# Block-diagonal attention keys: two masked copies in place of one broadcast product

## The chip, the cores and the metric

The kernel runs on one core of a Trainium2 chip. The metric is device time in microseconds (us), the median of three runs. A profiled execution gives the span of the program and, for each engine, what it did and waited for. TensorE does matmuls, VectorE and ScalarE work on what the matmuls leave in PSUM, GpSimd works on SBUF, and SyncE issues transfers. In the profile they are called PE (PEld for its weight loads), DVE, ACT, POOL and SP.

## The reference

The program normalises 2048 rows of 512 numbers and adds three things: the rows themselves, a sliding-window attention with 32 heads of only 16 numbers each, and a gated layer whose two hidden products of 1792 are multiplied with each other.

```python
def _A_ref(x, wqkv, wo):
    B, S, D = x.shape
    H = 32; Dh = D // H; W = 256
    # q, k, v: [B, H, S, Dh] from x @ wqkv
    scores = jnp.einsum("bhqd,bhkd->bhqk", q, k) * (Dh ** -0.5)
    mask = (idx[:, None] - idx[None, :] >= 0) & (idx[:, None] - idx[None, :] < W)
    scores = jnp.where(mask[None, None], scores, -1e9)
    p = _softmax(scores, axis=-1)
    o = jnp.einsum("bhqk,bhkd->bhqd", p, v)
    return (o back to [B, S, D]) @ wo

def _B_ref(x, w_gate, w_up, w_down):
    return ((x @ w_gate) * (x @ w_up)) @ w_down

xn = _layernorm(x)
return x + _A_ref(xn, A_wqkv, A_wo) + _B_ref(xn, B_w_gate, B_w_up, B_w_down)
```

(Shortened: the two returns and the comment put in words or in one line what the reference spells out with einsum and reshape.)

## The kernel before

The rows are worked on in four chunks T of 512. Within a chunk, the 32 heads are in four groups c of eight, so that one projection of 128 output partitions holds eight heads of 16. Partitions 0 to 15 belong to the first head of a pair, 16 to 31 to the second, and so on.

The score matmuls work on 32 partitions, that is, on a pair of heads, and must not mix the two. For this the keys are laid out block-diagonally: for each block of 64 key positions the tile K has 128 columns, 64 for the first head of the pair and 64 for the second. Where the column belongs to one head, the partitions of the other head are zero. The mask is made once, at the start:

```python
podd = const.tile([128, 1], I32, name="podd")          # L104: (partition >> 4) & 1
nc.vector.tensor_scalar(out=podd[:], in0=pi[:], scalar1=4, scalar2=1,
                        op0=ALU.arith_shift_right, op1=ALU.bitwise_and)
self.pair = const.tile([128, 2], BF16, name="pair")     # column 0: even, column 1: odd
nc.vector.tensor_copy(out=self.pair[:, 1:2], in_=podd[:])
nc.vector.tensor_scalar(out=self.pair[:, 0:1], in0=self.pair[:, 1:2], scalar1=-1.0, scalar2=1.0,
                        op0=ALU.mult, op1=ALU.add)
```

The projection of queries and keys, sixteen times of each kind (four chunks, four groups):

```python
def proj_qk(self, T, c, is_k, ks=range(4), engine=None):
    ps = self.bank(ks, "qkp")                            # one PSUM bank, 128 x 512 f32
    for k in ks:
        nc.tensor.matmul(ps[:], ...)                     # L254
    if 3 not in ks:
        return
    if is_k:
        self.K[T, c] = self.kpool.tile([128, 1024], BF16, tag="K", name="K")
        k = self.work.tile([128, 512], BF16, tag="k", name="k")
        self.copy(k[:], ps[:], engine)                   # PSUM to SBUF; frees the bank
        nc.vector.tensor_tensor(                         # L262
            out=self.K[T, c].rearrange("p (j r n) -> p j r n", r=2, n=64), op=ALU.mult,
            in0=k.rearrange("p (j n) -> p j n", n=64).unsqueeze(2).to_broadcast([128, 8, 2, 64]),
            in1=self.pair.unsqueeze(1).unsqueeze(3).to_broadcast([128, 8, 2, 64]))
        self.book("dve", BOTH)
    else:
        self.Q[T, c] = self.qpool.tile([128, 512], BF16, tag="Q", name="Q")
        self.copy(self.Q[T, c][:], ps[:], engine)
```

Where the engine is not given, `copy` decides between ScalarE (L233) and VectorE (L235) from a book of costs that the program keeps while it is being built. `BOTH` is an entry of that book. It changes nothing on the chip directly, but it can change which engine a later copy is given to:

```python
EXP, MASK, BOTH, SUMS, DIVIDE, TURN, STATS = 8.7, 1.9, 2.9, 4.2, 8.2, 6.1, 4.2
COPY = dict(act=2.8, dve=3.2)

def copy(self, out, in_, engine=None):
    if engine is None:
        engine = min(COPY, key=lambda e: max(self.free[e], self.now) + COPY[e])
    self.book(engine, COPY[engine])
    if engine == "act":
        nc.scalar.activation(out=out, in_=in_, func=ACT.Copy)    # L233
    else:
        nc.vector.tensor_copy(out=out, in_=in_)                  # L235
```

Those who use the keys, and the others that matter here:

```python
# scores: 75 steps; K is the stationary operand, four pairs of heads at once
nc.tensor.matmul(S[:, e, col:col + n], lhsT=self.K[U, c][rows, keys], rhs=self.Q[T, c][rows, q:q + n], ...)   # L315
nc.scalar.activation(out=P[:, :, 0:col], in_=S[:, :, 0:col], func=ACT.Exp, scale=0.25)                        # L321
# the window's edge is cut on GpSimd (L161), the diagonal on VectorE:
self.nc.vector.tensor_tensor(out=v, in0=v, op=ALU.min, in1=self.diag...)                                      # L345
# values: two accumulators, each one PSUM bank
accs = [self.ps_m.tile([128, 512], F32, tag="M", name="acc") for _ in range(2)]
nc.tensor.matmul(accs[par][...], lhsT=v, rhs=P[rows, e, col:col + n], ...)                                    # L368
```

The pool `ps_m` has four PSUM banks, which projections, gate and up products (L397, L408), down products (L430, L436) and accumulators take in turn. S has the other four, as a single buffer. The order in which TensorE works is laid down by hand: score steps are spread evenly among the projections and the gated layer.

Of the kernel before, what the change touches and what calls it, by code (L numbers as in the profile page):

```python
# [7 lines left out]
BF16 = mybir.dt.bfloat16  # L8
F32 = mybir.dt.float32
I32 = mybir.dt.int32  # L10
ACT = mybir.ActivationFunctionType
ALU = mybir.AluOpType
# [16 lines left out]
PADS = {27: 110, 57: 150}  # L29
MASKED, FIRST_DIVIDE, SECOND_DIVIDE = 8, 8, 24  # L30
COPY = dict(act=2.8, dve=3.2)
EXP, MASK, BOTH, SUMS, DIVIDE, TURN, STATS = 8.7, 1.9, 2.9, 4.2, 8.2, 6.1, 4.2


class Kernel:
# [26 lines left out]
    def setup(self):  # L62
        nc, const, NT, NF = self.nc, self.const, self.NT, self.NF
        self.x = const.tile([128, NT, 512], BF16, name="x")
        self.Wqkv = const.tile([128, 4, 1536], BF16, name="Wqkv")
        self.Wo = const.tile([128, 4, 512], BF16, name="Wo")
        self.Wg = const.tile([128, 4, self.F], BF16, name="Wg")
        self.Wu = const.tile([128, 4, self.F], BF16, name="Wu")
        self.Wd = const.tile([128, NF, 512], BF16, name="Wd")
        xv = self.x_d.rearrange("(t p) d -> p t d", p=128)  # L70
        wq = self.w_d["qkv"].rearrange("(k p) n -> p k n", p=128)
        wg = self.w_d["g"].rearrange("(k p) n -> p k n", p=128)
        wu = self.w_d["u"].rearrange("(k p) n -> p k n", p=128)
        for lo, hi in ((0, 1), (1, 2), (2, 4)):
            nc.sync.dma_start(out=self.x[:, lo:hi, :], in_=xv[:, lo:hi, :])
        for lo in (1024, 512, 0):
            nc.sync.dma_start(out=self.Wqkv[:, :, lo:lo + 512], in_=wq[:, :, lo:lo + 512])
        h = self.F // 2
        for lo in (0, h):
            nc.sync.dma_start(out=self.Wg[:, :, lo:lo + h], in_=wg[:, :, lo:lo + h])  # L80
            nc.sync.dma_start(out=self.Wu[:, :, lo:lo + h], in_=wu[:, :, lo:lo + h])
            if lo == 0:
                nc.sync.dma_start(out=self.x[:, 4:8, :], in_=xv[:, 4:8, :])
        nc.sync.dma_start(out=self.Wd[:], in_=self.w_d["d"].rearrange("(f p) n -> p f n", p=128))
        wo = self.w_d["o"].rearrange("(c p) n -> p c n", p=128)
        for c in range(4):
            nc.sync.dma_start(out=self.Wo[:, c, :], in_=wo[:, c, :])
        for lo, hi in ((8, 10), (10, 12), (12, NT)):
            nc.sync.dma_start(out=self.x[:, lo:hi, :], in_=xv[:, lo:hi, :])

        warm = const.tile([128, 1], F32, name="warm")
        nc.vector.memset(warm[:], 0.0)
        nc.scalar.activation(out=warm[:], in_=warm[:], func=ACT.Exp)
        self.idle = const.tile([128, 128], BF16, name="idle")
        nc.vector.memset(self.idle[:], 0.0)
        self.keep_busy(40)
        ident = const.tile([128, 128], BF16, name="ident")
        nc.gpsimd.memset(ident[:], 0.0)
        nc.gpsimd.affine_select(out=ident[:], in_=ident[:], compare_op=ALU.not_equal, fill=1.0,
                                base=0, pattern=[[-1, 128]], channel_multiplier=1)  # L100
        self.ident = ident
        pi = const.tile([128, 1], I32, name="pi")
        nc.gpsimd.iota(pi[:], pattern=[[0, 1]], base=0, channel_multiplier=1)
        podd = const.tile([128, 1], I32, name="podd")  # L104
        nc.vector.tensor_scalar(out=podd[:], in0=pi[:], scalar1=4, scalar2=1,
                                op0=ALU.arith_shift_right, op1=ALU.bitwise_and)
        self.pair = const.tile([128, 2], BF16, name="pair")
        nc.vector.tensor_copy(out=self.pair[:, 1:2], in_=podd[:])
        nc.vector.tensor_scalar(out=self.pair[:, 0:1], in0=self.pair[:, 1:2], scalar1=-1.0, scalar2=1.0,
                                op0=ALU.mult, op1=ALU.add)  # L110
        self.mhalf = const.tile([128, 4], F32, name="mhalf")
        nc.gpsimd.memset(self.mhalf[:], -0.5)
        self.diag = const.tile([128, 64], BF16, name="diag")
        self.far = const.tile([128, 64], BF16, name="far")
        nc.gpsimd.memset(self.diag[:], BIG)
        nc.gpsimd.memset(self.far[:], BIG)
        for half in (slice(0, 64), slice(64, 128)):
            self.triangle(self.diag[half], True)
            self.triangle(self.far[half], False)
        self.xnT, self.Q, self.hT, self.OT = {}, {}, {}, {}  # L120
        self.K, self.V, self.VS = {}, {}, {}
        self.strips, self.parts, self.at = {}, {}, {}
        self.stock = []
        self.new_values()
# [124 lines left out]
    def proj_qk(self, T, c, is_k, ks=range(4), engine=None):  # L249
        nc = self.nc  # L250
        lo = 512 * is_k + 128 * c
        ps = self.bank(ks, "qkp")
        for k in ks:
            nc.tensor.matmul(ps[:], lhsT=self.Wqkv[:, k, lo:lo + 128], rhs=self.xnT[T][:, :, k, :],  # L254
                             start=(k == 0), stop=(k == 3))
# [3 lines that stand above are left out]
            self.K[T, c] = self.kpool.tile([128, 1024], BF16, tag="K", name="K")  # L259
            k = self.work.tile([128, 512], BF16, tag="k", name="k")  # L260
            self.copy(k[:], ps[:], engine)
            nc.vector.tensor_tensor(out=self.K[T, c].rearrange("p (j r n) -> p j r n", r=2, n=64), op=ALU.mult,  # L262
                                    in0=k.rearrange("p (j n) -> p j n", n=64).unsqueeze(2).to_broadcast([128, 8, 2, 64]),
                                    in1=self.pair.unsqueeze(1).unsqueeze(3).to_broadcast([128, 8, 2, 64]))
            self.book("dve", BOTH)
        else:
            self.Q[T, c] = self.qpool.tile([128, 512], BF16, tag="Q", name="Q")
            self.copy(self.Q[T, c][:], ps[:], engine)
# [404 lines left out]
```

## Time and profile before

| | before |
|---|---|
| median of three runs | 264.81 us (264.8 to 265.33) |
| span of the profiled execution | 263.1 us |
| mean granted TensorE clock | 0.999 |
| the key product (L262) | 16 times, 20.1 us of VectorE, 1262 ns mean |
| the matmul of 128x512 (L397) | 224 times, 380 ns mean in the record, one every 0.216 us (0.86 us for four) |
| PSUM copies on VectorE (L235, 128x512) | about 0.68 us each |
| PSUM copies on ScalarE (L233, 128x512) | about 0.60 us each |
| the exponential (L321) | 75 times, 1877 ns mean |

How to read it: the busy time of an engine is the time in which at least one of its instructions ran. Matmuls overlap in the records, which is why a single one lasts longer than the distance between two. A line such as `PE acc L368 <- DVE Q L235: 0.6, 1, 0.6` tells that the matmuls of line 368 waited for the VectorE instruction of line 235 that writes Q: 0.6 us in total, once, 0.6 us at the longest. In a timeline a line begins with the start and the length in us, and ends, in brackets, with the idle time of the engine before it and what ended it.

### The profile page before, as it was taken

Reading aid. Unit: us, or ns where it says so; the run is one execution under the profiler, and the core shown is the slowest. Engines: PE = TensorE matmul, PEld = TensorE weight load, DVE = VectorE, ACT = ScalarE, POOL = GpSimd, SP = SyncE. Lnnn points to the kernel's source line nnn. Section 1 sums busy time; section 2 is a strip of 40 time slices with the busy share of each in tenths; the row PEclk is TensorE's granted clock in tenths of the full one; section 3 lists DMA queues with packets and bytes.
Section 4 is the critical chain, followed back from the end, with each engine's and each line's share of the span. In section 5 each row is a group of like instructions: output and inputs, shape, how many; then the busy total and the mean of one; then the engine's idle time right before and its main releaser. Section 6 shows DMA issues by size and latency. Waiting matters only on the chain.

```text
span 263.1 us, 7719 instructions
## 1 busy us (share of the span) xinstructions
PE 257.9 (98%) x3170; PEld 118.5 (45%) x3170; DVE 187.9 (71%) x341; ACT 176.7 (67%) x143; POOL 123.8 (47%) x278
## 2 busy tenths in 40 slices
PE   8999999998999999999999999999999999999995
PEld 8434444443443544344544454434543445444453
DVE  6698888879945597568983759767995235977344
ACT  3477788888656876778776566867787546787500
POOL 6217342427456745237556644544664451464600
PEclk9999999999999999999999999999999999999999
DMA  6999921120002300002001310000100100000002
GB/s 204 376 354 340 265 29 20 24 47 1 2 20 42 100 5 0 4 0 47 2 2 40 82 41 5 0 0 16 36 2 0 42 21 22 5 0 2 1 2 82
DMA packets 19427, 15.05 MB, mean 57 GB/s; under 512 B 7360, under 2 KB 19392, under 8 KB 19392
## 3 DMA queue, kind: packets, MB, share of 16 engines
q1 hardware_dynamic: 18848, 14.26, 18.9%
q8 instruction: 26, 0.43, 0.7%
q10 hardware_dynamic: 544, 0.30, 0.4%
q14 instruction: 9, 0.07, 0.1%
HBM read 9.70 MB, written 2.10 MB: 45 GB/s over the span
## 4 chain that ended last, share of the span: by engine, by line
PE 94%; DVE 4%; issue 1%; ACT 0%
PE up L408 19%; PE gp L397 19%; PE psd L430 17%; PE S L315 9%; PE qkp L254 8%; PE acc L368 6%; PE vp L242 5%; PE psd L436 5%; PE L L430 2%; PE wps L130 2%; DVE K L262 1%; DVE k L235 1%; PE L L436 1%; DVE P L345 1%; PE L L368 0%
## 5 line engine op out<-in xcount | busy, mean ns | idle before, releaser
L321 ACT ACTIVATE P<-S 128x2048 bf16<-128x2048 f32 x75 | 140.8, 1877 | 50.2 <-PE S L315 43.2
L161 POOL TENSOR_SCALAR_AFFINE_SELECT P<-P 64x256 bf16<-64x256 bf16 x224 | 107.2, 479 | 117.7 <-ACT P L321 99.1
L397 PE MATMUL gp<-xnT,Wg 128*128 128x512 bf16 x224 | 60.1, 380 | 0.0
L408 PE MATMUL up<-xnT,Wu 128*128 128x512 bf16 x224 | 59.1, 380 | 0.0
L413 DVE TENSOR_TENSOR hT<-up,gsb 128x512 bf16<-128x512 f32 x56 | 38.2, 684 | 16.4 <-PE up L408 11.9
L430 PE MATMUL psd<-Wd,hT 128*128 128x512 bf16 (+1 forms) x210 | 48.0, 369 | 0.0
L345 DVE TENSOR_TENSOR P<-P,diag 128x512 bf16<-128x512 bf16 (+1 forms) x75 | 30.9, 412 | 5.9 <-ACT P L321 5.9
L430 PEld LDWEIGHTS <-hT 128*128 128x128 bf16 x238 | 21.3, 98 | 25.3 <-issue 3.5
L408 PEld LDWEIGHTS <-Wu 128*128 128x128 bf16 x224 | 20.4, 98 | 25.6 <-issue 3.4
L397 PEld LDWEIGHTS <-Wg 128*128 128x128 bf16 x224 | 20.3, 98 | 25.3 <-issue 3.3
L315 PE MATMUL S<-Q,K 32*128 32x320 bf16 (+4 forms) x720 | 29.9, 254 | 0.3 <-DVE K L262 0.3
L254 PE MATMUL qkp<-xnT,Wqkv 128*128 128x512 bf16 x128 | 29.9, 380 | 0.0
L233 ACT ACTIVATE gsb<-gp 128x512 bf16<-128x512 f32 x39 | 22.9, 597 | 8.1 <-PE gp L397 7.2
L315 PEld LDWEIGHTS <-K 32*128 32x128 bf16 x720 | 10.3, 92 | 31.1 <-issue 30.3
L374 DVE STREAM_TRANSPOSE at<-acc 128x512 f32<-128x512 f32 x30 | 19.1, 686 | 5.2 <-PE acc L368 5.2
L262 DVE TENSOR_TENSOR K<-k,pair 128x1024 bf16<-128x1024 bf16 x16 | 20.1, 1262 | 2.0 <-ACT k L233 1.7
L446 DVE TENSOR_TENSOR x<-psd,x 128x512 bf16<-128x512 f32 (+1 forms) x15 | 9.7, 655 | 15.6 <-PE psd L436 15.6
L254 PEld LDWEIGHTS <-Wqkv 128*128 128x128 bf16 x128 | 11.7, 98 | 14.6 <-issue 1.8
L368 PE MATMUL acc<-P,V 64*32 64x320 bf16 (+4 forms) x672 | 17.7, 253 | 0.6 <-DVE Q L235 0.6
L368 PE MATMUL acc<-P,VS 64*32 64x320 bf16 (+4 forms) x672 | 17.7, 253 | 0.4 <-DVE k L235 0.4
L368 PEld LDWEIGHTS <-V 64*32 64x32 bf16 x720 | 15.2, 91 | 2.9 <-issue 2.5
L242 PE MATMUL vp<-Wqkv,xnT 128*128 128x512 bf16 x64 | 15.3, 380 | 0.0
(53 smaller groups left out, 183.1 us busy)
## 6 DMA issues: line engine op xcount, KB each, us to landing
out_dram<-x SPq DMA_DIRECT2D x15, 128.0 KB, 1.9
Wg<-in_B_w_gate_dram SPq DMA_DIRECT2D x2, 896.0 KB, 11.4
Wu<-in_B_w_up_dram SPq DMA_DIRECT2D x2, 896.0 KB, 12.7
Wd<-in_B_w_down_dram SPq DMA_DIRECT2D x1, 1792.0 KB, 17.3
Wqkv<-in_A_wqkv_dram SPq DMA_DIRECT2D x3, 512.0 KB, 6.2
x<-in_A_x_dram SPq DMA_DIRECT2D x2, 512.0 KB, 9.2
VS<-V SPq DMA_DIRECT2D x6, 144.0 KB, 2.6
x<-in_A_x_dram SPq DMA_DIRECT2D x3, 256.0 KB, 6.6
```

The lines of the kernel that those rows point to most:

```text
L161: nc.gpsimd.affine_select(out=v, in_=v, pattern=pattern + [[1 if diag else -1, 64]], compare_op=ALU.is_ge if diag else ALU.is_gt, fill=0.0 ...
L233: nc.scalar.activation(out=out, in_=in_, func=ACT.Copy)
L242: nc.tensor.matmul(ps[:], lhsT=self.xnT[T][:, b, k, :], rhs=self.Wqkv[:, k, 1024:1536], start=(k == 0), stop=(k == 3))
L254: nc.tensor.matmul(ps[:], lhsT=self.Wqkv[:, k, lo:lo + 128], rhs=self.xnT[T][:, :, k, :], start=(k == 0), stop=(k == 3))
L315: nc.tensor.matmul(S[:, e, col:col + n], lhsT=self.K[U, c][rows, keys], rhs=self.Q[T, c][rows, q:q + n], start=True, stop=True, tile_posit ...
L321: nc.scalar.activation(out=P[:, :, 0:col], in_=S[:, :, 0:col], func=ACT.Exp, scale=0.25)
L345: self.nc.vector.tensor_tensor(out=v, in0=v, op=ALU.min, in1=self.diag.unsqueeze(1).unsqueeze(1).to_broadcast([128, 4, n, 64]))
L368: nc.tensor.matmul(accs[par][32 * e:32 * e + 32, q:q + n], lhsT=v, rhs=P[rows, e, col:col + n], start=(i == 0), stop=(i == len(todo) - 1), ...
L397: nc.tensor.matmul(ps[:], lhsT=self.Wg[:, k, 128 * f:128 * f + 128], rhs=self.xnT[T][:, :, k, :], start=(k == 0), stop=(k == 3))
L408: nc.tensor.matmul(ps[:], lhsT=self.Wu[:, k, 128 * f:128 * f + 128], rhs=self.xnT[T][:, :, k, :], start=(k == 0), stop=(k == 3))
L413: nc.vector.tensor_tensor(out=self.hT[T, f][:], in0=ps[:], in1=self.gsb[:], op=ALU.mult)
L430: nc.tensor.matmul(ps, lhsT=self.hT[T, f][:, 128 * b:128 * b + 128], rhs=self.Wd[:, f, c0:c1], start=(f == 0), stop=False)
```

## The change

The product of the keys with a broadcast mask is replaced by two operations with one tensor input each. One multiplies the 512 columns by a per-partition scalar that is 1 for the partitions of even heads and 0 for the others, and writes the first 64 of every 128 columns of K. The other does so with the opposite scalar, for the other 64. What K holds is the same. It is meant to let VectorE do the step with operations that have a single tensor input and no broadcast operand. The two masks are kept as separate float columns, and the entry in the book of costs goes from 2.9 to 3.4.

```diff
-EXP, MASK, BOTH, SUMS, DIVIDE, TURN, STATS = 8.7, 1.9, 2.9, 4.2, 8.2, 6.1, 4.2
+EXP, MASK, BOTH, SUMS, DIVIDE, TURN, STATS = 8.7, 1.9, 3.4, 4.2, 8.2, 6.1, 4.2
@@ setup
-        self.pair = const.tile([128, 2], BF16, name="pair")
-        nc.vector.tensor_copy(out=self.pair[:, 1:2], in_=podd[:])
-        nc.vector.tensor_scalar(out=self.pair[:, 0:1], in0=self.pair[:, 1:2], scalar1=-1.0, scalar2=1.0,
+        self.odd = const.tile([128, 1], F32, name="odd")
+        nc.vector.tensor_copy(out=self.odd[:], in_=podd[:])
+        self.even = const.tile([128, 1], F32, name="even")
+        nc.vector.tensor_scalar(out=self.even[:], in0=self.odd[:], scalar1=-1.0, scalar2=1.0,
                                 op0=ALU.mult, op1=ALU.add)
@@ proj_qk
-            nc.vector.tensor_tensor(out=self.K[T, c].rearrange("p (j r n) -> p j r n", r=2, n=64), op=ALU.mult,
-                                    in0=k.rearrange("p (j n) -> p j n", n=64).unsqueeze(2).to_broadcast([128, 8, 2, 64]),
-                                    in1=self.pair.unsqueeze(1).unsqueeze(3).to_broadcast([128, 8, 2, 64]))
+            pair = self.K[T, c].rearrange("p (j r n) -> p j r n", r=2, n=64)
+            for par, mask in enumerate((self.even, self.odd)):
+                nc.vector.tensor_scalar(out=pair[:, :, par, :], in0=k.rearrange("p (j n) -> p j n", n=64),
+                                        scalar1=mask[:, 0:1], scalar2=None, op0=ALU.mult)
             self.book("dve", BOTH)
```

Built with the new number in the book, four PSUM copies change engines. In the second chunk's projection, a copy of k goes from VectorE to ScalarE and a gate copy from ScalarE to VectorE. In the last chunk's projection, a copy of Q goes from VectorE to ScalarE and a copy of k the other way. The orders of instructions of TensorE and of GpSimd are the same in both kernels.

## The prediction

> **What bounds the kernel now.** I read the shares of busy time first, then the chain, then the waits of TensorE, then the two stretches of the timeline in which such a wait stands.
>
> ```profile
> PE 257.9 (98%) x3170; PEld 118.5 (45%) x3170; DVE 187.9 (71%) x341; ACT 176.7 (67%) x143; POOL 123.8 (47%) x278
> ...
> PE 94%; DVE 4%; issue 1%; ACT 0%
> ```
>
> TensorE is busy for 257.9 of 263.1 us, and 94% of the chain that ended last is matmuls. VectorE, which the change works on, is at 71% and holds 4% of the chain. So the first limit on any gain is the 5.2 us in which TensorE has nothing to do. The waits of TensorE, with columns total us, times, longest us, account for 2.4 of them:
>
> ```profile
> PE wps L130 <- DVE idle L95: 1.1, 1, 1.1
> PE acc L368 <- DVE Q L235: 0.6, 1, 0.6
> PE acc L368 <- DVE k L235: 0.4, 1, 0.4
> PE S L315 <- DVE K L262: 0.3, 1, 0.3
> ```
>
> The first is the start of the program, before any key exists. The rest of the 5.2, about 2.8 us, is the tail after the last matmul (the last addition and store). Neither is touched. Only the other three waits, some 1.3 us, are behind VectorE work near the keys. They occur once each, at 13.65 us and at about 64 us. The timeline there (start us, length us, engine, line):
>
> ```profile
> 10.90 2.75 PE L254 MATMUL qkp<-xnT,Wqkv 128*128 128x512 bf16 x12
> ...
> 12.69 1.23 DVE L262 TENSOR_TENSOR K<-k,pair 128x1024 bf16<-128x1024 bf16 x1
> ...
> 13.97 0.40 PE L315 MATMUL S<-Q,K 32*128 32x192 bf16 x8 [0.32 <-DVE K L262]
> ```
>
> The projections end at 10.90 + 2.75 = 13.65, the key product at 13.92, and the first score matmul starts at 13.97: a direct wait of 0.32 us for the product, with 0.05 us from its end to the start.
>
> ```profile
> 60.62 1.88 ACT L321 ACTIVATE P<-S 128x2048 bf16<-128x2048 f32 x1 [0.23 <-PE S L315]
> 60.80 2.57 DVE L262 TENSOR_TENSOR K<-k,pair 128x1024 bf16<-128x1024 bf16 x2
> ...
> 63.29 0.62 DVE L345 TENSOR_TENSOR P<-P,diag 128x512 bf16<-128x512 bf16 x1
> 63.57 0.12 PEld L315 LDWEIGHTS <-K 32*128 32x128 bf16 x8 [0.42 <-issue]
> ...
> 63.83 0.68 DVE L235 CAST Q<-qkp 128x512 bf16<-128x512 f32 x1
> ...
> 64.43 0.68 DVE L235 CAST k<-qkp 128x512 bf16<-128x512 f32 x1
> 64.56 0.24 PE L368 MATMUL acc<-P,V 64*32 64x128 bf16 x4 [0.60 <-DVE Q L235]
> ...
> 65.16 0.24 PE L368 MATMUL acc<-P,VS 64*32 64x128 bf16 x4 [0.36 <-DVE k L235]
> ```
>
> Here the queue on VectorE is two key products, the diagonal mask, the copy of Q, the copy of k. TensorE wants two of the four PSUM banks for its accumulators; they still hold the projections that those two copies empty. It waits 0.60 + 0.36 = 0.96 us, at one remove behind 2.57 us of key products.
>
> [...] the median of the key product is 1226. The diagonal mask, whose two inputs both advance, has 415 ns as its median[...]. [...] The four selects beside the two products at 62.57 us took 2.57 us, or 0.64 each, against the mean of 0.479; other VectorE work ran there too[...].
>
> **The change part by part.**
>
> *Removed:* 16 products of 1.262 us mean, 20.2 us of VectorE.
>
> *Added:* 32 masked copies of 512 columns. [...] The nearest row of the trace is the normalisation (TENSOR_SCALAR, 512 bf16 columns, two per-partition scalars): median 412 ns, minimum 382[...]. The change itself books 3.4 units for the two; a PSUM copy books 3.2 and takes 0.689 us, so a unit is 0.215 us and the two are booked at 0.73 us. I choose 0.37 us for one, 0.74 for a pair, of which the sum is 11.8 us.
>
> *Net on VectorE:* 20.2 - 11.8 = 8.4 us less[...].
>
> *Off the path:* nearly all of it. Twelve of the 16 key tiles stand in stretches where TensorE waits for nobody, and VectorE merely becomes idle there.
>
> *On the path, first place:* the pair ends at 12.69 + 0.74 = 13.43, and with 0.05 the scores could start at 13.48, before TensorE is free at 13.65. [...] All of the 0.32 us goes.
>
> *On the path, second place:* the two products become 1.48 us instead of 2.57, and the product at 55.12 before them gets shorter too. The masking step then waits for the exponential, which ends at 60.62 + 1.88 = 62.50. With 0.05 and the mask at 0.62, the Q copy runs from 63.17 to 63.85, and the bank is free at 63.90. TensorE comes at 63.57 + 0.40 = 63.97. So the 0.60 goes, with only 0.07 to spare. The other bank held the k copy: the new number in the cost book moves that copy from VectorE to ScalarE, behind the exponential (62.50 + 0.60 = 63.10), so the 0.36 goes too. In exchange one gate copy moves to VectorE, to some 64.6 to 65.3; its bank is next wanted at about 66, by the next gate product. In the last projection a k copy and a Q copy change engines the other way. TensorE's order of instructions is the same in both kernels.
>
> *Sum:* 0.32 + 0.60 + 0.36 = 1.28 us. For the small margin I give back about 0.1: 264.81 - 1.2 = 263.6 us, 0.45% less.
>
> **The rivals.**
>
> First, *a gain in proportion to VectorE's saving*, some 8 us, to about 256. It would need VectorE to be the bound. Against it: the 98% of TensorE, and that its idle time within the run is only 1.3 us. It's excluded unless busy matmuls hide waits, since their ends are modelled.
>
> Second, *the wait changes its name*. At the second place the mask can't start before the exponential ends, so the Q copy is bound by ScalarE and no more by the keys. If the mask or the copy is 0.2 us later, or the moved gate copy holds its bank too long, some of the 0.96 us returns. The time would be 264.0 to 264.6.
>
> Third, *a collision triggered elsewhere*. The copies between engines and the arrival of everything 1 us earlier change how ScalarE, VectorE and GpSimd meet after 66 us; the schedule has hand-set shifts that fit the old one. For it: a gap of 1 us needs only one bank freed late. Against it: VectorE is less loaded everywhere, and no wait of TensorE after 66 us is among the rows above. It would make 265 to 266.
>
> Fourth, *the masked copies are slow* [...]. Then [...] the time is 265 or a little above. The normalisation at 412 ns, same operation and size, speaks against it; its output has no gaps, which the new one has, so I keep a small chance for it.
>
> **Range and chances.** The full gain is the floor: 263.5, and somewhat lower if the modelled ends hide a few tenths. No gain is 264.8, and the third or fourth rival adds up to half a microsecond. Eight in ten I put between 262.9 and 265.1. For 2%, 5.3 us would have to come or go: more than all the TensorE idle time that the change can reach, so within 2% is nearly certain.
>
> **What would show it.** In the changed profile: [...] VectorE busy near 179.5 us; TensorE still at about 258 us busy; no wait of the scores for the keys at 13.65; the accumulators near 63 us starting without a wait of 0.60 or 0.36. The prediction is wrong if a new wait of TensorE of over 0.3 us stands anywhere after 66 us, if masked copies take over 0.6 us, or if the span falls by much more than TensorE's idle time did.

## The result

The changed kernel takes 263.31 us (six runs, 263.23 to 263.45) against 264.81 us before (264.59 to 265.33 over six). The ratio is 0.9941, with an interval of 0.9928 to 0.9954: a small gain, clear of noise, and near the 263.6 us predicted. In the lines of the changed kernel, L255 is the projection, L265 the masked copies, L317 the scores, L370 the values, and L234 and L236 the PSUM copies on ScalarE and VectorE.

From the page of the changed kernel, the shares of busy time and the chain by engine:

```profile
PE 255.8 (98%) x3154; PEld 118.0 (45%) x3170; DVE 179.5 (69%) x357; ACT 176.4 (68%) x143; POOL 116.0 (44%) x278
...
PE 98%; issue 1%; DVE 0%
```

VectorE lost 8.4 us of busy time, and its share of the chain fell from 4% to 0%; the time fell by 1.5 us. The groups of the masked copies (busy us, mean ns), and then the same instructions with minimum, median and maximum:

```profile
L265 DVE TENSOR_SCALAR K<-k,even 128x512 bf16<-128x512 bf16 x16 | 6.5, 405 | 3.5 <-ACT k L234 3.1
L265 DVE TENSOR_SCALAR K<-k,odd 128x512 bf16<-128x512 bf16 x16 | 6.5, 404 | 0.0
```

```profile
L265 DVE TENSOR_SCALAR K<-k,even x16: 352/354/583, 12.6 to 190.3; 128x512 bf16<-128x512 bf16 x16
L265 DVE TENSOR_SCALAR K<-k,odd x16: 332/348/557, 12.8 to 190.6; 128x512 bf16<-128x512 bf16 x16
```

The waits of TensorE in the changed kernel (total us, times, longest us) no longer hold a wait for VectorE after the start of the program:

```profile
PE wps L131 <- DVE idle L95: 1.1, 1, 1.1
PE psd L432 <- issue: 0.6, 4, 0.2
PE L L432 <- issue: 0.2, 1, 0.2
PE psd L438 <- issue: 0.2, 1, 0.2
PE vp L243 <- issue: 0.2, 1, 0.2
```

The `issue` rows name no instruction waited for, and add no step to the comparison that follows. They come from the record: the trace holds 3154 matmuls instead of 3170 for the same program, and has 16 gaps of 0.05 to 0.16 us, one for each that is missing, 1.7 us in all. With them TensorE is busy for some 257.5 us, and not for the 255.8 us of the page.

TensorE does the same instructions in the same order in both kernels, so the two timelines can be laid side by side. I took the start of each of the 75 score steps in both and subtracted. The difference is 0.52 us at the first step, 0.52 to 0.54 up to the seventeenth, 1.77 at the eighteenth, and 1.77 or 1.78 from there to the last. The whole gain arises in two places. The timeline of the changed kernel at both (start us, length us):

```profile
10.76 2.75 PE L255 MATMUL qkp<-xnT,Wqkv 128*128 128x512 bf16 x12
...
12.55 0.35 DVE L265 TENSOR_SCALAR K<-k,even 128x512 bf16<-128x512 bf16 x1
...
12.82 0.35 DVE L265 TENSOR_SCALAR K<-k,odd 128x512 bf16<-128x512 bf16 x1
...
13.45 0.40 PE L317 MATMUL S<-Q,K 32*128 32x192 bf16 x8
```

```profile
60.09 1.88 ACT L323 ACTIVATE P<-S 128x2048 bf16<-128x2048 f32 x1 [0.19 <-PE S L317]
...
61.12 0.41 DVE L347 TENSOR_TENSOR P<-P,diag 128x512 bf16<-128x512 bf16 x1
61.45 0.68 DVE L236 CAST Q<-qkp 128x512 bf16<-128x512 f32 x1
61.87 0.59 ACT L234 ACTIVATE k<-qkp 128x512 bf16<-128x512 f32 x1
...
63.04 0.40 PE L317 MATMUL S<-Q,K 32*128 32x192 bf16 x8
...
63.37 0.24 PE L370 MATMUL acc<-P,V 64*32 64x128 bf16 x4
63.38 0.24 PE L370 MATMUL acc<-P,VS 64*32 64x128 bf16 x4
```

From the start of these projections to the first scores, TensorE needs 13.45 - 10.76 = 2.69 us; before it was 13.97 - 10.90 = 3.07. That is 0.38 us gained. The other 0.14 of the 0.52 arose upstream, before any key existed, and differs from execution to execution: in the last experiment below, whose program is the same up to there, the projections begin at 11.96 us and not at 10.76. At the second place the two accumulator groups start 0.33 and 0.34 us after the scores' start instead of 0.99 and 1.59. That is 1.25 us, which agrees with the step in the score starts, 1.77 - 0.53 = 1.24. Together the two places make 1.62 us, beside the 1.50 us between the medians.

### The profile page after: what moved, and what is told of

Its sections match the earlier page's. It is cut to its first block, busy times and chain, and to the rows that moved or that the text cites. A ratio compares the mean times of both kernels' runs of the same rounds, so it can differ in the third digit from the quotient of the medians.

```text
span 261.2 us, 7718 instructions
## 1 busy us (share of the span) xinstructions
PE 255.8 (98%) x3154; PEld 118.0 (45%) x3170; DVE 179.5 (69%) x357; ACT 176.4 (68%) x143; POOL 116.0 (44%) x278
## 4 chain that ended last, share of the span: by engine, by line
PE 98%; issue 1%; DVE 0%
PE gp L399 19%; PE up L410 19%; PE psd L432 17%; PE qkp L255 11%; PE S L317 10%; PE acc L370 7%; PE vp L243 5%; PE psd L438 5%; PE L L432 2%; PE wps L131 2%; PE L L438 1%; PE xTp L213 0%; PE L L370 0%; DVE x L448 0%; DVE idle L95 0%
## 5 line engine op out<-in xcount | busy, mean ns | idle before, releaser
L162 POOL TENSOR_SCALAR_AFFINE_SELECT P<-P 64x256 bf16<-64x256 bf16 x224 | 99.7, 445 | 123.7 <-ACT P L323 108.6
L432 PE MATMUL psd<-Wd,hT 128*128 128x512 bf16 (+1 forms) x202 | 46.9, 369 | 0.8 <-issue 0.6
L347 DVE TENSOR_TENSOR P<-P,diag 128x512 bf16<-128x512 bf16 (+1 forms) x75 | 29.6, 394 | 5.9 <-ACT P L323 5.9
L317 PE MATMUL S<-Q,K 32*128 32x320 bf16 (+4 forms) x720 | 29.8, 254 | 0.1
L255 PE MATMUL qkp<-xnT,Wqkv 128*128 128x512 bf16 x128 | 29.9, 380 | 0.0
L234 ACT ACTIVATE gsb<-gp 128x512 bf16<-128x512 f32 x38 | 22.3, 596 | 7.7 <-PE gp L399 6.9
L317 PEld LDWEIGHTS <-K 32*128 32x128 bf16 x720 | 10.3, 92 | 30.7 <-issue 30.3
L255 PEld LDWEIGHTS <-Wqkv 128*128 128x128 bf16 x128 | 11.7, 98 | 14.7 <-issue 1.8
L370 PE MATMUL acc<-P,VS 64*32 64x320 bf16 (+4 forms) x672 | 17.7, 253 | 0.0
L370 PE MATMUL acc<-P,V 64*32 64x320 bf16 (+4 forms) x672 | 17.5, 253 | 0.0
L370 PEld LDWEIGHTS <-V 64*32 64x32 bf16 x720 | 15.1, 91 | 2.3 <-issue 1.7
L370 PEld LDWEIGHTS <-VS 64*32 64x32 bf16 x720 | 14.7, 91 | 0.6 <-issue 0.2
```

The lines of the kernel that those rows point to most:

```text
L162: nc.gpsimd.affine_select(out=v, in_=v, pattern=pattern + [[1 if diag else -1, 64]], compare_op=ALU.is_ge if diag else ALU.is_gt, fill=0.0 ...
L370: nc.tensor.matmul(accs[par][32 * e:32 * e + 32, q:q + n], lhsT=v, rhs=P[rows, e, col:col + n], start=(i == 0), stop=(i == len(todo) - 1), ...
L432: nc.tensor.matmul(ps, lhsT=self.hT[T, f][:, 128 * b:128 * b + 128], rhs=self.Wd[:, f, c0:c1], start=(f == 0), stop=False)
```

## The experiments

Unless it is said otherwise, the differences below are those of score starts against the kernel before, which can be read to about 0.02 us. The diffs are shortened, with words in brackets in place of code; kernels with both forms make both kinds of mask at the start. Chunk 0 begins the program, and chunk 1's keys are made around 53 to 64 us.

### Which part of the edit: the copies or the book

The first kernel has the masked copies and the old number.

```diff
-EXP, MASK, BOTH, ... = 8.7, 1.9, 3.4, ...
+EXP, MASK, BOTH, ... = 8.7, 1.9, 2.9, ...      # changed kernel, old number
```

> The masked copies with the old number (2.9) in the cost book, so no PSUM copy changes its engine. My theory: the bank of the second waited-for accumulator is freed in time even if VectorE copies that k itself, since VectorE reaches it about 1 us earlier; both waits of 0.60 and 0.36 us in chunk 1 stay away and the time is that of the change, 263.3 us (263.1 to 263.6). Rival (the moved copies bring part of the gain): a wait of about 0.36 us comes back in chunk 1 and the time is 263.7 or more.

Measured: 263.05 us, ratio 0.9931 (0.9910 to 0.9953), the same as the changed kernel within the intervals. The step in chunk 1 is 1.24 us. No wait came back; the rival falls.

The second has the broadcast product and the new number.

```diff
-EXP, MASK, BOTH, ... = 8.7, 1.9, 2.9, ...
+EXP, MASK, BOTH, ... = 8.7, 1.9, 3.4, ...      # kernel before, new number
```

> The broadcast product with the new number (3.4) in the book: only the PSUM copies change engines. My theory: the wait for the k copy (0.36 us) goes, as ScalarE takes that copy, and the wait for the Q copy (0.60) and that of the first scores (0.32) stay; 264.4 us, between 264.1 and 264.7. Rival (the book number is most of the gain): 263.6 or less.

Measured: 264.12 us, ratio 0.9974 (0.9961 to 0.9986), at the near end of the range. One step, 0.58 us, in chunk 1. Among the waits of TensorE the other two remain, and the k copy's is gone:

```profile
PE acc L368 <- DVE Q L235: 0.6, 1, 0.6
PE S L315 <- DVE K L262: 0.3, 1, 0.3
```

So the book's number alone removes the second of the three waits, and does it by moving one PSUM copy. With fast masked copies it is not needed. The parts overlap and do not add up.

### Where it arises: one chunk at a time

Three kernels keep the product and the old number, and use the masked copies in some chunks only.

```diff
+            if T == 0:          # then T == 1, then T > 1
+                (the two masked copies)
+            else:
                 (the broadcast product)
```

> Masked copies in chunk 0 alone, the product in chunks 1 to 3, old book. My theory: only the direct wait of the first scores goes; from the first score step on TensorE is 0.3 to 0.4 us earlier relative to the start of its projections than before, and this difference stays constant to the end; 264.4 us. Rival (VectorE's time counts as such): a quarter of the saved VectorE time, about 2 us, is gained, 262.8 us.

Measured: 264.21 us, ratio 0.9982 (0.9970 to 0.9995). From projections to scores 13.49 - 10.81 = 2.68 us, so 0.39 gained; the difference from the kernel before stays between 0.48 and 0.50 from the first step to the last, of which 0.09 is the earlier start of the projections. The rival of 2 us falls.

> Masked copies in chunk 1 alone, old book. My theory: the two accumulator waits near 64 us go, and with them the broken overlap of the first matmuls after each, 1.24 us in all, in one step between the scores of 63.6 us and those of 67.5 us; wait of the first scores (0.32) stays; 263.6 us (263.3 to 263.9). Rival (proportion): 2 us. Rival (only the recorded 0.96 us is gained): a step of 0.96 us.

Measured: 263.44 us, ratio 0.9944 (0.9930 to 0.9958). One step, from -0.13 to 1.11: 1.24 us. The rival of 0.96, which was the term of my sum, falls.

> Masked copies in chunks 2 and 3 alone, old book: half of the saved VectorE time, none of it where TensorE waits. My theory: no change of the time, 264.8 us (within 0.2), with VectorE some 4 to 5 us less busy, and the score steps at the same distance from those of before all along. Rival (proportion): 264.8 - 4 = 260.8 us, or any gain of over 0.4 us.

Measured: 264.75 us against 264.76, ratio 1.000 (0.9992 to 1.0008). VectorE is 4.2 us less busy (183.7 us instead of 187.9), GpSimd 5.6 us (118.27 instead of 123.85), and the score starts differ by 0.03 us at most. Here half of the change is worth nothing.

### What a masked copy costs

```diff
+ group 0: four copies of 256 columns        + group 1: scalar1=0.5 in place of the mask
+ group 2: output K[:, 512*par : 512*par+512] + group 3: scalar1=mask, scalar2=mask
```

In groups 1 and 2 the keys are then not what the reference needs; only the durations are read.

> The changed kernel with other forms of the masked copy by head group, which change what K holds in groups 1 and 2: group 0 four copies of 256 columns instead of two of 512; group 1 a constant 0.5 in place of the per-partition mask; group 2 the output without gaps; group 3 two per-partition scalars in one copy. To tell what makes a copy 0.35 us long. [...] If the per-partition scalar costs time, the constant form is about 0.06 us shorter and the form with two about 0.06 us longer (0.41, as the normalisation). If the gaps cost, the dense form is shorter. I expect [...] 0.06 us for each per-partition scalar and nothing for the gaps. The time itself stays within 0.5 us of 263.3, whatever the forms.

The one run took 263.02 us. The masked copies by form (minimum, median, maximum ns): L268 is group 0, L272 group 1, L276 group 2, L280 group 3.

```profile
L268 DVE TENSOR_SCALAR K<-k,even x8: 274/284/381, 12.5 to 181.8; 128x256 bf16<-128x256 bf16 x8
...
L272 DVE TENSOR_SCALAR K<-k x8: 285/293/529, 14.2 to 184.0; 128x512 bf16<-128x512 bf16 x8
L276 DVE TENSOR_SCALAR K<-k,even x4: 353/454/579, 16.4 to 185.4; 128x512 bf16<-128x512 bf16 x4
...
L280 DVE TENSOR_SCALAR K<-k,even x4: 412/414/579, 18.6 to 190.3; 128x512 bf16<-128x512 bf16 x4
```

In the changed kernel the masked copies beside GpSimd's selects take up to 0.58 us (see below), so the minimum of the four dense copies is the number to take: 353, as with gaps (352). Against the 354 that is the median in the changed kernel, half the columns take 354 - 284 = 70 ns less, a constant in place of the per-partition scalar 354 - 293 = 61 ns less, and two such scalars 414 - 354 = 60 ns more. So of a copy's 354 ns some 140 go with its 512 columns (an estimate, twice the 70), about 60 with its scalar, and none with the gaps. The normalisation's 412 ns is what the form with two scalars takes here (414).

### How much room there is: adding work instead of taking it away

If VectorE's time is worth nothing in chunks 2 and 3, adding some there ought to cost nothing up to a point. Here I was wrong.

```diff
             if T < 2:
                 (the two masked copies)       # changed kernel
             else:
+                for _ in range(2):
                     (the broadcast product)   # twice, the same values
```

> The changed kernel, but in chunks 2 and 3 the broadcast product is done twice over (the second writes the same values again): some 15 us more of VectorE than in the changed kernel. My theory: the slack is finite; the copies of Q behind the products release their banks about 2 us late for the accumulators of chunks 2 and 3, so one or two waits of TensorE of 1 to 2 us appear in each of the two chunks and nothing elsewhere: 265.5 to 268 us. Rival (VectorE has room enough): 263.3. Rival (VectorE's time counts as such): 278.

Measured: 276.45 us, ratio to before 1.0453 (1.0430 to 1.0476), far outside my range and near the rival of VectorE's time. But it isn't spread evenly. Against the changed kernel, the score starts lose 7.53 us around the accumulators of chunk 2 and 3.95 us around those of chunk 3, and nothing elsewhere. Waits of TensorE in this kernel (L380 is the values, L357 the diagonal mask, L386 the transposes of the accumulators, L259 the projection, L240 the PSUM copies on VectorE):

```profile
PE acc L380 <- DVE P L357: 3.5, 2, 1.9
PE qkp L259 <- DVE at L386: 2.5, 1, 2.5
PE acc L380 <- DVE k L240: 1.5, 1, 1.5
...
PE acc L380 <- DVE Q L240: 0.5, 1, 0.5
```

I had followed the PSUM copies only. They are the smaller part. Behind the last products in VectorE's queue stand the diagonal mask that the value matmuls wait for, and the transposes that free the accumulators' own banks for the last projection. And in chunk 2 the clock fell during the waits. By stretches (from:to, length, then busy us and count of PE, PEld, DVE, ACT, POOL, then the granted clock, DMA share and GB/s):

```profile
127.00:128.00 1.00, 0.00 (x0) 0.00 (x0) 1.00 (x2) 0.00 (x0) 1.00 (x1) 1.00 0.00 0
128.00:129.00 1.00, 0.63 (x16) 0.32 (x16) 1.00 (x2) 0.00 (x0) 0.94 (x2) 1.00 0.00 0
129.00:130.00 1.00, 0.00 (x0) 0.00 (x0) 0.96 (x2) 0.94 (x1) 0.94 (x2) 0.84 0.00 0
130.00:131.00 1.00, 0.00 (x0) 0.00 (x0) 1.00 (x2) 0.93 (x1) 1.00 (x1) 0.50 0.00 0
...
135.00:136.00 1.00, 1.00 (x3) 0.29 (x2) 0.92 (x2) 0.60 (x1) 0.00 (x0) 0.50 0.00 0
136.00:137.00 1.00, 1.00 (x15) 0.24 (x14) 0.22 (x1) 0.00 (x0) 0.00 (x0) 0.75 0.00 0
```

TensorE worked 0.63 us in some 4.7, and its granted clock fell from 1.00 to 0.50. It stayed there for most of the 5.1 us from 131.42, when TensorE had work again, to about 136.5 (an estimate from the 0.75 between 136 and 137), and was 1.00 from 137. From the last projection to the next scores it takes 5.18 us here, and 2.68 in the next experiment, where TensorE waited 2.02 us ahead of the same projection and the clock stayed at 1.00: I put the 2.5 us of difference down to the clock. How much idle time it takes for the clock to fall was not shown. I expected a smaller addition to find the room.

```diff
                 (the broadcast product)       # kernel before, all chunks
+            if T > 1:
+                (the two masked copies as well)
```

> The kernel before, but in chunks 2 and 3 the product is followed by the two masked copies as well (the same values again): 8 times 0.62 us, some 5 us more of VectorE than before, a dose between the single and the doubled product. My theory: VectorE's room in these chunks is used up by about this amount, and a wait of 0 to 1 us appears in each of the two chunks; no fall of the clock, as no idle stretch gets near the 4.7 us of the doubled product. 264.8 to 266.8 us. Rival (VectorE's time counts as such, as the 13 us of the doubled product suggest): 269 to 270 us.

Measured: 269.57 us, ratio 1.0197 (1.0166 to 1.0228). Wrong again, and in the rival's range: the steps are 2.86 us in chunk 2 and 1.65 in chunk 3, together 4.5 for 5.0 us more of VectorE's busy time (192.9 instead of 187.9). The clock stayed at 1.00. I gave up the idea of room, and looked at VectorE's queue in the kernel before, chunk 2 (start, length; brackets would show an idle time):

```profile
119.92 1.23 DVE L262 TENSOR_TENSOR K<-k,pair 128x1024 bf16<-128x1024 bf16 x1
121.06 0.69 DVE L235 CAST k<-qkp 128x512 bf16<-128x512 f32 x1
121.78 1.23 DVE L262 TENSOR_TENSOR K<-k,pair 128x1024 bf16<-128x1024 bf16 x1
122.93 0.63 DVE L345 TENSOR_TENSOR P<-P,diag 128x512 bf16<-128x512 bf16 x1
...
124.08 1.30 DVE L262 TENSOR_TENSOR K<-k,pair 128x1024 bf16<-128x1024 bf16 x1
125.30 0.49 DVE L345 TENSOR_TENSOR P<-P,diag 128x256 bf16<-128x256 bf16 x1
125.71 1.21 DVE L262 TENSOR_TENSOR K<-k,pair 128x1024 bf16<-128x1024 bf16 x1
126.85 2.50 DVE L374 STREAM_TRANSPOSE at<-acc 128x512 f32<-128x512 f32 x4
```

VectorE has no pause from 119.20 us to the end of the transposes at 129.35, though its share over the whole span is 71%. The projection that waits for a transposed bank starts at 127.76, and the first of the four transposes (0.70 us long by itself) ends at 126.85 + 0.70 = 127.55. The schedule just fits. Two more runs test this reading.

```diff
+            if T > 1:
+                (the even masked copy as well)      # kernel before
```

> The kernel before with one more masked copy (the even half again) after each product of chunks 2 and 3: 8 times some 0.3 us, half the dose of the run before. New theory, after the two larger doses: VectorE works in these two stretches without a pause, and TensorE reaches it with almost no room to spare, so that what is added there comes out of TensorE nearly in full, while what is taken away there is worth nothing. Then half the dose costs nearly half: steps of about 1.2 us in chunk 2 and 0.8 us in chunk 3, 266.3 to 267.3 us. Rival (a room of 1 us or more before anything is lost): 264.8 to 265.5.

Measured: 266.15 us, ratio 1.0059 (1.0042 to 1.0076), a little under my range. Steps of 1.05 us in chunk 2 and 0.58 in chunk 3. VectorE is busy for 2.1 us more than before (190.0 instead of 187.9), and 1.63 us are lost: there is some room, a few tenths per chunk, and after it nearly everything counts.

```diff
                 (the two masked copies)             # changed kernel
+            if T > 1:
+                (the two masked copies again)
```

> The changed kernel with each masked copy of chunks 2 and 3 done twice: the same 5 us of VectorE that cost 4.7 us when they were added to the kernel before. New theory: the change has made just this much room in those stretches (8 times 0.6 us), so they now cost almost nothing: 263.3 to 263.8 us. Rival (added VectorE time there always costs, room or not): 267 to 268 us.

Measured: 263.00 us, ratio to before 0.9946 (0.9928 to 0.9965), as the changed kernel. VectorE is 4.1 us busier than there (183.6 instead of 179.5), and the only step after the first scores is the 1.24 us of chunk 1. The work that cost 4.5 us on top of the products costs nothing on top of the copies.

## Why the prediction was right

**What bounds the kernel:** right. TensorE is still busy for 98%, and the gain stayed within the 5.2 us in which it had nothing to do. The first rival, 8 us in proportion to VectorE's saving, is excluded by the copies in chunks 2 and 3, which saved 4.2 us for nothing. But "VectorE merely becomes idle there" hid that these stretches were close to being bound by VectorE. The 71% of the whole span told nothing of it.

**Cost of the parts:** the total came out exact, 8.4 us less and VectorE at 179.5 us; a pair is a little better than the chosen 0.74. The second copy starts 0.27 us after the first, so an undisturbed pair takes 0.62 us, half of the product's 1.226, and the fourth rival, slow masked copies, falls. The choice of 0.37, an estimate from the 0.73 booked for two, was right in size: a copy's median is 0.35 us, of which about 60 ns go with its scalar. Why the product takes 1.226 us was not shown, as no run changed its broadcast alone.

**First place:** the wait goes, 0.38 us instead of 0.32.

**Second place:** the waits go, but the term was mis-sized at 0.96 us, and measured 1.24. The idle times of a page are counted from the modelled end of the matmul before. Without a wait, a group starts before the end of its predecessor in the record: 0.07 us before the scores' end, and the second group 0.01 us after the first group's start. The cost of the waits is the difference from start to start, 0.66 and 0.59 us, and not the 0.60 and 0.36 of the brackets. The kernel with the new book and the old product confirms it: it removed one bracket of 0.36 us and gained 0.58. The prediction had named this, "somewhat lower if the modelled ends hide a few tenths", but did not put it in its sum.

**The margin of 0.07 us:** wrong. I took the diagonal mask as waiting for the exponential that ran beside it. In the changed kernel the mask starts at 61.12 us, before that exponential ends at 60.09 + 1.88 = 61.97; it belongs to an earlier step. The Q copy ends at 62.13, well over a microsecond before its bank is wanted. So the second rival, a wait that changes its name, did not come up, and the 0.1 us that I gave back for it was not owed.

**Collisions after 66 us:** none. The difference of the score starts is constant to 0.01 us over the last 57 steps.

**The other copy in the book:** the gate copy on VectorE ended at 64.14, before its bank was wanted at 65.20, as worked out.

## What to carry to other kernels

The engine that bounds the whole sets how much can be gained; which queue it waits for is read at the wait, and what the wait is worth is read from start to start. An engine with much idle time on average (VectorE here, busy for 71%) can be without a pause for ten microseconds (119.20 to 129.35) just where the bounding engine needs it. There, work taken away may be worth nothing (4.2 us less, no gain) while about as much added costs nearly in full (5.0 us more, 4.5 lost), so a saving of no effect on the time can still be worth having as room for later changes.

## What the hardware showed that I had not expected

GpSimd's selects can be much longer beside the broadcast product (up to 1.32 us), and hardly so beside the masked copies alone (up to 0.50). The selects at the second place, before and after (start, length, count):

```profile
62.57 2.57 POOL L161 TENSOR_SCALAR_AFFINE_SELECT P<-P 64x256 bf16<-64x256 bf16 x4 [0.27 <-ACT P L321]
```

```profile
62.04 1.84 POOL L162 TENSOR_SCALAR_AFFINE_SELECT P<-P 64x256 bf16<-64x256 bf16 x4 [1.25 <-ACT P L323]
```

The median of all selects is 0.414 us in both kernels. The four after take 0.41 each, with short pauses between them, though two of them run beside masked copies; of the four before, the first takes 1.07 us. Over the whole traces, 13 selects run beside products for more than half of their time: the nine that start while one runs take 1.07 to 1.32 us, the four that start before it 0.41. A select that has only masked copies beside it takes 0.41 to 0.50. In the other direction, masked copies that run beside selects take up to 0.58 us, and those with nothing of GpSimd beside them 0.33 to 0.36. In all GpSimd became 7.8 us less busy, 116.0 instead of 123.8, without one instruction less. No experiment here set product and select alone beside each other, so the cause of the longer selects and copies was not shown.

Chunk 2 loses nearly twice as much as chunk 3 to the same added work, 2.86 against 1.65 us. In the kernel before, all four products of chunk 2 stand ahead of the transposes (shown above), and only three of chunk 3. With product and copies, the transposes (L384) begin at 129.78 and 193.97 us:

```profile
187.62 1.30 DVE L262 TENSOR_TENSOR K<-k,pair 128x1024 bf16<-128x1024 bf16 x1
188.85 0.28 DVE L345 TENSOR_TENSOR P<-P,diag 128x256 bf16<-128x256 bf16 x1
189.05 2.50 DVE L374 STREAM_TRANSPOSE at<-acc 128x512 f32<-128x512 f32 x4
...
192.16 1.23 DVE L262 TENSOR_TENSOR K<-k,pair 128x1024 bf16<-128x1024 bf16 x1
```

```profile
129.78 2.49 DVE L384 STREAM_TRANSPOSE at<-acc 128x512 f32<-128x512 f32 x4
...
193.97 2.50 DVE L384 STREAM_TRANSPOSE at<-acc 128x512 f32<-128x512 f32 x4
```

Counted from the scores ahead of them (0.10 us earlier than before in chunk 2, 2.76 later in chunk 3), they begin 3.03 and 2.16 us later than before; in chunk 3, TensorE waits for the diagonal mask just ahead of them, which is later by the same 2.16. Less the losses that leaves a room of 0.17 and 0.51 us, the few tenths found above. This is read from the traces, and no run moved a product from one side of the transposes to the other.
